# A planner that groups cache loads: later grouping, a constant for short transfers, and pairs for the free heads' values

## The chip, the core and the metric

The kernel runs on one core of one Trainium2 chip. The metric is device time in microseconds (us) of one execution. The core has TensorE (PE in the profile; its weight loads are listed apart as PEld), VectorE (DVE), ScalarE (ACT), GpSimd (POOL) and SyncE (SP). SP computes nothing here: it issues nearly all the transfers, one after the other, and waits before an issue until the place that the transfer will fill is free.

## What is computed

Four residual layers follow one another on eight sequences (batch rows) of one token each: attention over a cache, an MLP with a shift between the rows, and both again.

```python
x = A_x                                            # 8 rows of 448
x = x + A(layernorm(x), k_cache, v_cache, wq, wo)  # 16 query heads on 8 cached heads, 4096 keys, width 256
x = x + B(layernorm(x), w1, w2, w3, w4)            # MLP; also mixes neighbouring rows
x = x + A(layernorm(x), k_cache, v_cache, wq, wo)  # the same caches and weights
x = x + B(layernorm(x), w1, w2, w3, w4)
```

With one token in a row, the shift of B takes its values from outside the sequence, which are zeros; so every row goes through all four layers alone. A cached head of one row holds 4096 x 256 bf16 numbers, 2 MB for its keys and 2 MB for its values. All heads of all rows are 256 MB, and both attention layers need them.

## The kernel before, in words

**Tiles and places.** A head's keys or values lie in SBUF as four units ("quarters") of 512 KB, which are 4096 bytes in each of 128 partitions. `kv` has places for 30 quarters (`QUARTERS`), and everything streams through them. Heads 0 to 2 of a row are called free (`free_heads`): they are loaded afresh in each layer. Heads 3 to 7 are partly kept: of their keys 17 quarters, and of their values 7, stay in `kv` from the first attention layer to the second of the same row. 24 of 30 places are then taken, and six are left for the stream.

**Order of the work.** The row loop `for b in range(B)` interleaves the second layer of row b with the first layer of row b+1. For each row there is a stretch in which `mid` (the MLP of row b and the queries of its second layer) runs as a serial chain of small PE and DVE operations, while the values of the free heads of row b+1 pass through the six places. I call it the value stage. It comes seven times between rows, and the last rows end in a stretch of the same kind. After it the second layer's score operations (PE L1135) release kept keys, and more places come free.

**Operations of one quarter.** `front` transposes keys on PE (L1481, four at a time), copies them out of PSUM (DVE L1412 or ACT L1413) and scores them (L1135, or L1377 for whole rows of scores). `back` multiplies values with the softmax weights: eight matmuls of L1261 for a quarter, here called its PV. A quarter's last reader (the PV of a value quarter, the score of a key quarter) frees its place (`o.frees`).

**The planner.** `Plan.schedule` runs while the program is being built. It simulates all engines with costs in us and writes down one fixed instruction order for each. Nothing of it runs on the chip; on the chip each instruction waits on semaphores for those it depends on, and each engine takes its instructions in the written order. SP's order is fixed in advance (`prio`), but the planner decides how many neighbouring quarters of a head go in one transfer and which places they get. That is `next_kv`: `u.most` limits the group, it looks for a run of neighbouring free places of that length, and it accepts a later time for it up to

```python
late = max(free["sp"], dma_end - self.LEAD)
```

where `dma_end` is the planned end of all the transfers issued so far. When no such run comes in time, it takes the longest run that there is at that moment. A planned transfer starts at the earliest `ISSUE` = 4.0 us after its issue (`start = max(t + self.ISSUE, dma_end)`), and its duration is set in `issue_kv` (L644). The grouped transfer has one semaphore: the PV of its first quarter waits until the whole group has landed. A transfer for several places waits for the last of their former readers.

**Group limits.** In `back`, `most` is `MOST` for values of the free heads of rows 1 to 7 in the first layer, `MOST2` for one head of the second layer, and 4 otherwise. With `MOST = 1` the values of the free heads come as single quarters.

**Fillers.** Where the planned PE idles, the planner inserts matmuls without use (`warm`, L1686), if a count of recent columns is below a limit. There are 398 of them in the program.

Of the kernel before, what the change touches and what calls it, by code (L numbers as in the profile page):

```python
# [35 lines left out]
BOOST = None  # L36
HOTK = 7
L2 = (3, 4, 2, 1, 0)
MOST = 1
MOST2 = 4  # L40
BACKS = (0, 1, 3)
STAT_AT = 4
# [9 lines left out]
ST = 504  # L52
Q1 = 176
ROWS = True


class Op:
# [28 lines left out]
class Plan:  # L86
# [5 lines left out]
    HOT = 3500  # L92


    ISSUE, LEAD = 4.0, 5.0
    BLOCK, FETCH = 128, 6.0
    LAT = {"pe": 0.25, "dve": 0.06, "act": 0.06, "pool": 0.05, "sp": 0.4}

# [374 lines left out]
def bass_interleave_layers__gqa_block_cached__mixer_s_mlp__decode_kernel(  # L473
# [146 lines left out]
    FASTER = 1.05  # L620
# [15 lines left out]
    def issue_kv(o, n, q):  # L636

        (cache, b, h), u = o.unit.tile, o.unit.u
        src = cache[b, h].rearrange("(m s) d -> m (s d)", m=P)[:, u * 2048:(u + n) * 2048]
        dst = kv[:, q * 2048:(q + n) * 2048]  # L640
        slot_n[q] += 1
        o.emit = lambda eng: eng.dma_start(dst, src)
        o.dma = (slot_sem[q], 16 * slot_n[q])
        o.dur = ((n << 15) / 26.88e3 + 8 * 0.008) / FASTER  # L644

    plan.issue_kv = issue_kv

# [454 lines left out]
    def front(layer, b, h, prio=None):  # L1102
# [37 lines left out]
        def score_op(u, ss, where_of, keys):  # L1140
# [4 lines left out]
                           prio=prio and prio + len(plan.ops))  # L1145
        rows = ROWS and not last_head and not (layer and h == first2[b])
        by_rows[layer, b, h] = rows
# [87 lines left out]
    def back(layer, b, h):  # L1235
# [11 lines left out]
        fresh_v = [u for u in range(4) if u not in vs]  # L1247
        most = MOST if (layer == 0 and b and h in free_heads) else MOST2 if h == l2_heads[1] and layer else 4
        if (layer, b, h) == (1, B - 1, free_heads[-1]):
# [496 lines left out]
```

## Time and profile before

| | |
|---|---|
| three runs | 1083.20, 1088.74, 1092.21 us; median 1088.74 |
| profiled execution, its own time | 1083.66 us |
| its span, first to last instruction | 1081.5 us |
| mean granted TensorE clock | 0.923 |
| busy: PE, DVE, ACT, POOL | 944.7, 600.1, 338.3, 98.3 us |
| moved by DMA | 436.37 MB, mean 403 GB/s |
| transfers of `kv`: quarters, pairs, triples, fours | 219, 16, 15, 128 |

The last row adds up the key and value lines of the profile's list of DMA issues (512, 1024, 1536 and 2048 KB). A profile page cuts the span into 40 slices of 27 us and gives each the busy tenths of an engine, the granted clock and the moved GB/s. "To landing" is the time from the issue of a transfer by SP to the semaphore event that says that all of it has arrived; a transfer that stands behind others in the queue has a long one.

### The profile page before, as it was taken

How to read it: one execution, taken by the hardware profiler on the slowest of the kernel's cores; microseconds unless marked ns; L12 is line 12 of the kernel's file. 1: busy time of each engine (PE TensorE's matmuls, PEld its weight loads, DVE VectorE, ACT ScalarE, POOL GpSimd, SP SyncE). 2: the span in 40 equal slices, each digit the busy share in tenths (PEclk: the TensorE clock that was granted, in tenths of full speed). 3: DMA queues.
4: the chain of work that ended last, by engine and by line, in shares of the span. 5: the costliest groups of instructions: out<-in, count | busy, mean ns of one | idle time of the engine just before them, and what ended most of it. 6: DMA issues, size and time to landing. Idle time of an engine off the chain costs nothing.

```text
span 1081.5 us, 33945 instructions
## 1 busy us (share of the span) xinstructions
PE 944.7 (87%) x15116; PEld 650.5 (60%) x15116; DVE 600.1 (55%) x1896; ACT 338.3 (31%) x939; POOL 98.3 (9%) x278
## 2 busy tenths in 40 slices
PE   4988798998988988988999988889898898898795
PEld 3656556665656656666566665657565675566563
DVE  3345455554656556555565555565565665565564
ACT  1245023351223403353133421344122341243140
POOL 0000010000100101011010100000010000111010
PEclk9899989998999969999699998999899997999796
DMA  9999999999999999999999999999999999999994
GB/s 369 408 426 422 392 399 427 423 421 395 403 425 425 417 399 410 424 426 415 378 423 425 425 411 394 428 423 423 397 392 428 424 404 404 401 428 417 338 374 176
DMA packets 58973, 436.37 MB, mean 403 GB/s; under 512 B 6334, under 2 KB 9548, under 8 KB 38092
## 3 DMA queue, kind: packets, MB, share of 16 engines
q1 hardware_dynamic: 58740, 433.95, 98.0%
q8 instruction: 118, 1.93, 0.7%
q10 hardware_dynamic: 88, 0.26, 0.1%
q14 instruction: 27, 0.22, 0.1%
HBM read 434.18 MB, written 0.01 MB: 401 GB/s over the span
## 4 chain that ended last, share of the span: by engine, by line
DMA 52%; PE 37%; DVE 6%; issue 2%; ACT 1%; SPq 0%; POOL 0%; POOLq 0%; DVEq 0%
DMA kv<-in_A_k_cache_dram 32%; DMA kv<-in_A_v_cache_dram 19%; PE psT L1481 14%; PE psP L1261 7%; PE psT L1377 5%; PE psM L1135 3%; PE psR L1311 2%; PE psM L890 2%; DMA w3x_sb<-in_B_w_dram 1%; DVE oS L1277 1%; PE psP L1686 1%; DVE oS L1275 1%; DVE kv L1412 1%; PE psP L1285 1%; PE psM L1052 1%
## 5 line engine op out<-in xcount | busy, mean ns | idle before, releaser
L1481 PE MATMUL psT<-ident_f,kv 128*128 128x128 f32 x2752 | 381.6, 286 | 28.5 <-DMA kv<-in_A_k_cache_dram 26.5
L1481 PEld LDWEIGHTS psT<-ident_f,kv 128*128 128x128 f32 x2752 | 307.7, 145 | 109.6 <-issue 59.8
L1412 DVE COPY kv<-psT 128x512 f32<-128x512 f32 x377 | 258.4, 691 | 187.7 <-PE psT L1481 182.7
L1413 ACT COPY kv<-psT 128x512 f32<-128x512 f32 x343 | 199.9, 587 | 411.6 <-PE psT L1481 317.7
L1261 PE MATMUL psP<-kv,pT 128*2 128x256 bf16 x4096 | 181.2, 293 | 20.8 <-DMA kv<-in_A_v_cache_dram 18.4
L1377 PE MATMUL psT<-kv,qz 128*32 128x512 bf16 x1664 | 132.5, 394 | 4.3 <-ACT kv L1413 2.0
L1261 PEld LDWEIGHTS psP<-kv,pT 128*2 128x2 bf16 x4096 | 83.3, 83 | 66.2 <-DMA kv<-in_A_v_cache_dram 31.2
L1215 POOL PARTITION_ALL_REDUCE gm<-pm x128 | 45.5, 356 | 761.9 <-DVE pm L1213 748.0
L1225 ACT ACTIVATE pT<-sS,nb,fac 128x32 bf16<-128x32 bf16 x128 | 52.6, 417 | 96.8 <-DVE nb L1219 96.8
L1275 DVE CAST oS<-psP 128x256 bf16<-128x256 f32 x128 | 54.0, 422 | 49.9 <-PE psP L1261 48.6
L1311 PE MATMUL psR<-wo_sb,oT 128*1 128x448 bf16 x444 | 67.7, 389 | 4.3 <-DVE oT L1291 2.4
L1229 POOL PARTITION_ALL_REDUCE Db<-rs x128 | 51.2, 400 | 186.5 <-ACT pT L1225 186.5
L1285 PE MATMUL psP<-sel,oS 128*128 128x2 bf16 x512 | 32.1, 166 | 33.8 <-DVE oS L1277 32.1
L1285 PEld LDWEIGHTS psP<-sel,oS 128*128 128x128 bf16 x512 | 23.4, 99 | 63.4 <-DVE oS L1277 60.7
L1225 ACT ACTIVATE pT<-sS,nb 128x32 bf16<-128x32 bf16 x128 | 40.7, 325 | 58.9 <-DVE nb L1219 58.9
L1377 PEld LDWEIGHTS psT<-kv,qz 128*32 128x32 bf16 x1664 | 34.1, 95 | 39.2 <-issue 10.9
L1392 DVE CAST sr<-psT 128x512 bf16<-128x512 f32 x58 | 40.1, 691 | 29.4 <-PE psT L1377 29.1
L1277 DVE TENSOR_TENSOR oS<-psP,oS 128x256 bf16<-128x256 f32 x128 | 54.1, 423 | 3.2
L1686 PE MATMUL psP<-ident_f 128*128 128x256 bf16 x331 | 51.7, 283 | 0.0
L1135 PEld LDWEIGHTS psM<-qz,kv 128*128 128x128 bf16 x1344 | 41.9, 100 | 14.8 <-issue 5.4
L1135 PE MATMUL psM<-qz,kv 128*128 128x48 bf16 x1344 | 48.5, 188 | 1.4 <-DVE qz L1532 0.3
L1208 DVE CAST sS<-psM 128x64 bf16<-128x64 f32 x128 | 28.0, 219 | 33.4 <-PE psM L1135 25.7
(191 smaller groups left out, 777.2 us busy)
## 6 DMA issues: line engine op xcount, KB each, us to landing
kv<-in_A_k_cache_dram SPq DMA_DIRECT2D x68, 2048.0 KB, 23.0
kv<-in_A_v_cache_dram SPq DMA_DIRECT2D x60, 2048.0 KB, 17.2
kv<-in_A_v_cache_dram SPq DMA_DIRECT2D x182, 512.0 KB, 7.7
kv<-in_A_k_cache_dram SPq DMA_DIRECT2D x37, 512.0 KB, 7.8
kv<-in_A_k_cache_dram SPq DMA_DIRECT2D x11, 1536.0 KB, 17.8
kv<-in_A_v_cache_dram SPq DMA_DIRECT2D x11, 1024.0 KB, 8.7
kv<-in_A_v_cache_dram SPq DMA_DIRECT2D x4, 1536.0 KB, 9.9
kv<-in_A_k_cache_dram SPq DMA_DIRECT2D x5, 1024.0 KB, 9.6
```

What stands on the lines that cost most here:

```text
L1135: last = t.matmul(ps[:, SB + 2 * i:SB + 2 * i + 2 * REP], a()[:, c:256:2], bcast(rhs(c), REP, 1), start=(c == 0), stop=(c == 1))
L1225: return a.activation(pT[nr][:, :, :].rearrange("p i j -> p j i")[:, jj, :], sview[:, jj, :], ACT.Exp, bias=nb[nm][:, jj:jj + 1], scale=sc ...
L1261: last = t.matmul(ps[g4:g4 + 2, PV0:PV0 + DH], pT[nr][:, k, :], slot_ap(q, s * 256, 256), start=(i < 4), stop=(i >= 28), skip_group_check= ...
L1275: plan.op("dve", lambda v: v.tensor_copy(oS[:, 0, :], po), 0.36, "o", rd=[("pv", par, x) for x in range(4)], wr=["oS0"], banks=[bk], prio=hi)
L1277: plan.op("dve", lambda v: v.tensor_tensor(oS[:, 1, :], po, oS[:, 0, :], ALU.subtract), 0.36, "o", rd=["oS0"] + [("pv", par, x) for x in r ...
L1285: last = t.matmul(ps[:, PV1 + 2 * c:PV1 + 2 * c + 2], oS[:, w, c:DH:2], sel[:, :], start=(w == 0), stop=(w == 1))
L1311: last = t.matmul(psR[r:r + 1, 0:D], oT[no][:, i % 2, i // 2:i // 2 + 1], wo_sb[:, a:a + D], start=(k == 1 and i < 2), stop=(k == turn_at ...
L1377: last = t.matmul(psT[bank][32 * g:32 * g + 32, :], qz[:, a:a + 32], slot_ap(qs[g // 2], g % 2 * 1024, 1024)[:, c:1024:2], start=(half == ...
L1412: return e.tensor_copy(dst, psT[bank][:, :])
L1413: return e.copy(dst, psT[bank][:, :])
L1481: last = t.transpose(psT[bank][:, s * P:(s + 1) * P], src, ident_f[:, :])
L1686: return t.matmul(dst, ident_b, bcast(ident_b[:, 0:n // 4], 4, 1), start=True, stop=True)
```

## The change

Three numbers of the planner and the program are changed. `MOST` goes from 1 to 2, so that two quarters of a free head's values may go in one transfer. `LEAD` goes from 5.0 to 3.5, so that the planner waits for a longer run of free places until 3.5 us before the planned queue is empty. `SHORT`, a new constant of 0.1 us, is added to the planned duration of transfers of one or two quarters. No operation of the computation is added or taken away, and the bytes are the same; which quarters go together, the places, the order on all engines and the number of fillers follow from the planner.

```diff
-MOST = 1
+MOST = 2
 MOST2 = 4
...
 ROWS = True
+SHORT = 0.1
...
-    ISSUE, LEAD = 4.0, 5.0
+    ISSUE, LEAD = 4.0, 3.5
...
         o.emit = lambda eng: eng.dma_start(dst, src)
         o.dma = (slot_sem[q], 16 * slot_n[q])
-        o.dur = ((n << 15) / 26.88e3 + 8 * 0.008) / FASTER
+        o.dur = ((n << 15) / 26.88e3 + 8 * 0.008) / FASTER + SHORT * (n < 3)
```

## The prediction

> **What bounds the kernel now.** I read the page's slices and its DMA part first, then compared stretches, then looked at single waits.
>
> ```profile
> DMA  9999999999999999999999999999999999999994
> GB/s 369 408 426 422 392 399 427 423 421 395 403 425 425 417 399 410 424 426 415 378 423 425 425 411 394 428 423 423 397 392 428 424 404 404 401 428 417 338 374 176
> q1 hardware_dynamic: 58740, 433.95, 98.0%
> DMA 52%; PE 37%; DVE 6%; issue 2%; ACT 1%; SPq 0%; POOL 0%; POOLq 0%; DVEq 0%
> ```
>
> The DMA engines are busy from start to end, 98.0% of the span with SP's queue alone. PE's 37% of the chain that ended last is time in which a transfer was in flight too. So time is won or lost only where the stream slows: it moves 422 to 428 GB/s at best, and twice in about five slices it falls to some 395. The next view sets six value stages (262 to 916) beside four stretches of large transfers.
>
> ```profile
> 262.00:274.00 12.00, 11.48 (x236) 6.25 (x233) 7.36 (x41) 0.21 (x1) 0.00 (x0) 0.53 0.99 377
> 387.00:400.00 13.00, 12.12 (x260) 7.05 (x260) 7.01 (x41) 0.21 (x1) 0.00 (x0) 0.50 1.02 393
> 518.00:531.00 13.00, 12.26 (x258) 7.21 (x257) 7.42 (x42) 0.22 (x1) 0.00 (x0) 0.50 0.99 363
> 645.00:658.00 13.00, 11.24 (x266) 6.89 (x266) 7.17 (x42) 0.22 (x1) 0.00 (x0) 0.78 1.02 402
> 773.00:786.00 13.00, 11.70 (x262) 7.04 (x260) 6.81 (x40) 0.21 (x1) 0.00 (x0) 0.58 1.00 378
> 903.00:916.00 13.00, 12.29 (x273) 7.16 (x275) 6.92 (x41) 0.21 (x1) 0.00 (x0) 0.57 1.02 401
> ...
> 197.00:240.00 43.00, 40.22 (x438) 29.08 (x436) 24.67 (x59) 21.85 (x52) 4.13 (x11) 0.98 1.01 425
> 325.00:359.00 34.00, 30.60 (x346) 21.14 (x344) 22.09 (x53) 14.12 (x38) 3.38 (x9) 1.00 1.00 423
> 455.00:499.00 44.00, 40.09 (x447) 28.36 (x449) 24.99 (x60) 22.24 (x56) 4.36 (x12) 1.00 1.01 424
> 580.00:625.00 45.00, 42.08 (x468) 30.29 (x471) 25.81 (x64) 21.45 (x51) 4.06 (x11) 1.00 1.00 423
> ```
>
> The last three columns are granted clock, DMA share and GB/s. Weighted by length the value stages move 386 GB/s (363 to 402), the others 424. A quarter (0.524 MB) takes 1.36 us at the one rate and 1.24 at the other. The engines are not idle in the value stage (0.99 to 1.02); their packets are slower. PE has half its clock there in most windows.
>
> How full the queue is tells the time to landing: of the quarters issued in 387 to 400, then of all transfers of `kv`.
>
> ```profile
> DMA to landing us min/median/max: 6.5/6.7/7.2
> ...
> DMA to landing us min/median/max: 4.9/11.7/47.4
> ```
>
> The second line's 4.9 us is the shortest. Less a quarter's own 1.3 us (0.524 MB at 405 GB/s, below), some 3.6 us must lie queued ahead at its issue, or the stream has a hole. The stage has 6.7 - 1.3 = 5.4 us ahead: 1.8 us of cover. In the last stretch, 1003 to 1041, the cover fails:
>
> ```profile
> DMA  8979898999989999689999998312989999999999
> GB/s 280 289 285 293 293 276 250 410 375 401 388 293 341 306 289 302 267 358 392 392 431 423 440 384 345 121 56 60 224 233 332 388 336 388 418 401 427 423 423 474
> ```
>
> At 1027 to 1029 the engines fall to 1 to 3 tenths busy, while SP waits for a PV.
>
> **The change part by part.** The changed program's instruction order can be read without running it. It has 92 quarters, 57 pairs, 22 triples and 134 fours, 305 transfers for 378. So 127 quarter transfers go: 82 of these quarters come in pairs, 45 in triples and fours; the planner still finds no run of two places for many.
>
> *Size.* Between 124 and 134, where quarters stood deep in the queue (10.9 us to landing) at full clock, the stream made 405 GB/s: 1.295 us for a quarter, 0.056 over 1.239. I take that as the cost of being a quarter, the rest of 1.36 as that of a shallow queue. The pair's price is not seen apart; half-way, 0.028. Gain: 82 x 0.028 + 45 x 0.056 = **4.8 us**. The bounds: 0 if size costs nothing, and 127 x (1.358 - 1.239) = 15.1 us if all of the stage's slowness goes with size.
>
> The Trainium skill, DMA: Bandwidth & Descriptors, section Bandwidth, asks for transfers of at least 1 MiB for 75% of peak and gives 341 GB/s for one (measured with GpSimd issuing); an estimate from that page would price a quarter at over 1.54 us and raise the gain to some 38 us. The trace disagrees: queued quarters move 405.
>
> *Depth.* With six places, a quarter's issue waits for the PV of the quarter six before, so five quarters are ahead. In the old order 87 transfers wait with five ahead, three with four, one with three. In the new order 38 wait with five, 29 with four (18 of them pairs), three with three, one with two. One quarter less leaves 5.4 - 1.3 = 4.1 us ahead, 0.5 over the 3.6. A pair waits for two PVs, and at half clock 80 matmuls of L1261 took 6.3 us, 0.63 a quarter: 3.5 us ahead, no cover. The spread of the landing row is 0.7 us, so I price 0.2 us a pair and 0.05 a single: 18 x 0.2 + 11 x 0.05 = 4.1 us. Two pairs with three ahead lack a whole quarter: 2 x 1.3 = 2.6. Bounds: 0 (the 3.6 is an upper bound of what is needed) to the second rival's price.
>
> *The end.* At 386 GB/s the 12.55 MB of 1003 to 1041 would take 32.5 us instead of 38: 5.5 us lost to holes. The new order has its thinnest places there too (five ahead would be 6.5 us and are 5.4, so a release takes 1.1; two ahead are then 2.6 - 1.1 = 1.5 and lack 2.1 us, three ahead lack 0.8, and two waits behind transposes about 0.75 each): 4.4. Net -1.1, between -5.5 and +5.
>
> *Score waits.* At the end of each value stage the next quarters take places that scores (L1135) free. Before, each came when its own place was free; now a pair or triple waits for the last. SP's waits for L1135 are 73.1 us in 39 cases, 1.9 us each, under the queue. I price 0.5 us in each of seven stages, 3.5 in all, between 0 and two quarters' time, 2 x 1.3 x 7 = 18.2.
>
> *Fillers.* 488 instead of 398, 23 more in the value stages. The L1686 row has 283 ns or less for one. Outside the stages PE waits for DMA and they cost nothing; within, 23 x 0.283 = 6.5 us would be the price without cover. I take 1.
>
> *SP.* 73 issues less, about 0.33 us each, in the waiting time of an engine that computes nothing: 0. LEAD and SHORT run in no instruction; their effect is the order counted above. No other large part of the order changes: before, during and after, the fours of the key stretches have eight or more quarters ahead.
>
> Sum: -4.8 + 4.1 + 2.6 - 1.1 + 3.5 + 1 = **+5.3 us**. On the profiled execution's own 1083.66 (1081.5 of span) that is 1089.0. That execution lies at the low end of the three runs; on their median 1088.74 it is 1094.0. I forecast between: **1091 us**.
>
> **The rivals.**
> *Faster, the slowness goes with size.* Then 15.1 us return with no hole: 1068.6 by the execution, 1073.6 by the median; with half of it about 1079. For it: all slow slices are those with quarters. Against: quarters deep in the queue lost less than half of it, and the shallow stages have half the clock as well.
>
> *Slower, the queue runs dry.* Place: the pair's wait on two PVs in the value stage. It decides from the point where less than 3.6 us is queued ahead. If one PV more (0.63 us) is missing in each pair and half as much in each single: 18 x 0.63 + 11 x 0.3 = 14.6; with a whole quarter at each stage's score wait, 7 x 1.3 = 9.1, plus 2.6 and 1, less 4.8 and 1.1: +21.4, so 1105.1 by the execution and 1110 by the median. For it: the hole at 1027, and that PE is 86 to 96% busy in these stages at half clock. Against: the stage's landing times scatter by only 0.7 us. The Trainium skill (same page, Rules for kernel authors) says to issue a DMA early so that its fixed cost overlaps; pairs issue later, and by that rule this rival holds. The hole agrees with it.
>
> *The change hardly does what it says.* The order shows that it does in part; if pairs are as slow as quarters and the queue is still deep enough, it is the old time, within the forecast's class.
>
> **How the numbers follow.** A measurement of this kernel can tell about 1% (10.9 us) from no change. Forecast and the unchanged case, 1078 to 1099.6: 0.53. Queue dry, above: 0.32. Size, below: 0.15. The range takes most of both: 1077 to 1108.
>
> **What would show it.** Right: the list of issues with 92 quarters; value stages near 386 GB/s still; shortest landing of pairs near 3.6 + 2.5 us with small holes in the slices; the key stretches at 424. Size right: 405 or more in the value stages. Dry: DMA digits below 9 in each stage and long waits of SP for L1261 and L1135. Wrong altogether: a key stretch below 420, or a chain that ends on PE while the DMA idles.

## The result, and the profile after

The changed kernel takes 1095.36 us (median of 20 runs, 1089.34 to 1099.50), the kernel before beside it 1086.53 us (20 runs). The ratio is 1.0079, with a 95% interval of 1.0063 to 1.0094: some 8.6 us slower, within the 1% that the prediction called "same". The profiled execution has a span of 1094.1 us against 1081.5, which is 12.6 us; 4 us of that difference belong to these two executions and not to the kernels, so the accounting below, which is made on the two traces, explains more than the medians ask for.

First the slices, the queue and the chain of the changed kernel's page.

```profile
DMA  9999999999999999999999999999999999999894
GB/s 367 409 425 422 390 378 425 425 417 378 405 427 425 419 359 412 427 424 417 371 426 424 423 401 377 428 424 416 384 409 425 425 407 346 422 424 409 303 380 180
q1 hardware_dynamic: 48228, 433.95, 97.1%
DMA 53%; PE 34%; DVE 6%; SPq 4%; issue 1%; ACT 1%; POOL 0%; DVEq 0%
```

The best slices move 422 to 428 GB/s, as they did. The slow slices have become slower: 359, 371 and 346 stand where 399, 378 and 404 stood. A new entry in the chain is SP's queue with 4% (0 before); it is no measure of the loss, for `SHORT` alone (below) has 5% there without one, and experiment 5, which lost more, has 0%. The windows show where the time went. Six value stages stand first, four key stretches after them; the last three columns are again the granted clock, the DMA share and GB/s.

```profile
262.00:276.00 14.00, 13.49 (x296) 8.87 (x293) 7.03 (x42) 0.21 (x1) 0.00 (x0) 0.56 0.96 338
390.00:404.00 14.00, 13.30 (x281) 8.51 (x280) 7.19 (x43) 0.21 (x1) 0.00 (x0) 0.51 0.95 333
521.00:535.00 14.00, 13.49 (x293) 8.77 (x290) 7.13 (x42) 0.21 (x1) 0.00 (x0) 0.55 0.98 349
650.00:664.00 14.00, 13.82 (x295) 9.02 (x288) 7.24 (x42) 0.21 (x1) 0.00 (x0) 0.64 0.96 355
780.00:794.00 14.00, 13.09 (x301) 8.73 (x293) 7.36 (x43) 0.21 (x1) 0.00 (x0) 0.65 0.97 348
910.00:924.00 14.00, 12.94 (x322) 9.16 (x323) 7.32 (x42) 0.21 (x1) 0.00 (x0) 0.88 0.89 323
199.00:242.00 43.00, 40.03 (x440) 28.87 (x438) 24.31 (x60) 22.61 (x56) 4.24 (x12) 1.00 1.00 423
328.00:361.00 33.00, 30.23 (x345) 21.09 (x344) 22.10 (x53) 13.69 (x35) 3.36 (x9) 1.00 1.01 425
459.00:502.00 43.00, 38.69 (x426) 27.20 (x425) 23.61 (x58) 21.52 (x52) 4.12 (x11) 1.00 1.00 423
585.00:630.00 45.00, 40.56 (x445) 29.74 (x443) 23.88 (x58) 20.71 (x50) 3.76 (x10) 0.96 1.00 423
```

The key stretches are what they were (423 to 425). The value stages fell from a mean of 386 GB/s to 341, and their DMA share from 0.99 to 1.02 down to 0.89 to 0.98: before, the packets were slow but the engines never idle; now the engines idle as well. One stage seen closely, 388 to 417, in 40 slices of 0.7 us:

```profile
DMA  9999879899979989699999898999999999999998
GB/s 384 446 373 412 333 271 277 362 395 463 305 226 373 373 339 339 249 328 350 316 345 260 294 384 271 356 418 390 379 429 345 379 458 362 345 401 424 367 441 356
```

There is no single hole, but nine small ones: 6 to 8 tenths busy again and again. The same view of the kernel before (385 to 412) shows 9 in all slices but one. The times to landing, of the transfers issued in 390 to 404 and then of all of `kv`, say the same:

```profile
DMA to landing us min/median/max: 5.4/6.4/7.4
...
DMA to landing us min/median/max: 4.0/13.3/47.6
```

The shortest landing fell from 4.9 to 4.0 us. In 390 to 404 three pairs (median 6.9 us) and four quarters (6.0) are listed. Less the pair's own 2.5 us, a pair has 4.4 us ahead of it; the stage before had 5.4. The list of issues has 92 quarters (72 of values, 20 of keys), as the order said.

**An account of the stream.** A transfer's landing less the landing of the one before it is its spacing. Where more than 6 us are queued ahead, the median spacing is 1.273 us for a quarter, 2.49 for a pair, 3.72 for a triple and 4.909 for a four, which is 1.227 for each of its quarters. What a transfer lands later than that I call its hole. It is "thin" where less than 5.2 us were queued ahead at its issue, and belongs to a PV or a score by the operation that the written order makes it wait for. Loads of weights that land between two transfers of `kv` are no hole. In us, from issue and landing times of the two traces (number of transfers in brackets):

| | before | after | difference |
|---|---|---|---|
| size: median spacings over 1.227 a quarter | 11.3 | 7.2 | -4.1 |
| thin, PV, value stages to 1003 us | 0.8 (8) | 18.6 (41) | +17.8 |
| thin, score, up to 1003 us | 2.0 (11) | 1.9 (6) | -0.1 |
| thin, from 1003 us to the end | 5.5 (4) | 10.1 (6) | +4.6 |
| all others | 25.4 | 19.2 | -6.2 |
| sum | 45.1 | 57.1 | +12.0 |

The sum is 12.0 of the 12.6 us of span. The last row is mostly number as well: a transfer with more than 6 us queued ahead lands some 0.06 us later on average than at the median, in both kernels (17.5 us in 273 transfers, 12.1 in 224), and there are fewer of them. With mean spacings in place of medians (1.321, 2.509, 3.766, 4.989) the size row is -8.6, and the last row is smaller in the same measure.

### The profile page after: what moved, and what is told of

The parts are those of the page before. It is cut to its first block, busy times and chain, and to the rows that moved or that the text cites. A ratio compares the mean times of both kernels' runs of the same rounds, so it can differ in the third digit from the quotient of the medians.

```text
span 1094.1 us, 34048 instructions
## 1 busy us (share of the span) xinstructions
PE 946.7 (87%) x15206; PEld 654.1 (60%) x15206; DVE 596.8 (55%) x1891; ACT 342.3 (31%) x944; POOL 97.9 (9%) x278
## 3 DMA queue, kind: packets, MB, share of 16 engines
q8 instruction: 119, 1.95, 0.7%
## 4 chain that ended last, share of the span: by engine, by line
DMA 53%; PE 34%; DVE 6%; SPq 4%; issue 1%; ACT 1%; POOL 0%; DVEq 0%
DMA kv<-in_A_k_cache_dram 31%; DMA kv<-in_A_v_cache_dram 22%; PE psT L1482 10%; PE psP L1262 7%; PE psT L1378 4%; SPq L643 4%; PE psM L1136 3%; PE psR L1312 2%; PE psM L891 2%; PE psP L1687 1%; DVE oS L1276 1%; DVE oS L1278 1%; PE psM L1053 1%; SPq L626 1%; PE psP L1286 1%
## 5 line engine op out<-in xcount | busy, mean ns | idle before, releaser
L1482 PE MATMUL psT<-ident_f,kv 128*128 128x128 f32 x2752 | 371.3, 282 | 27.6 <-DMA kv<-in_A_k_cache_dram 25.4
L1482 PEld LDWEIGHTS psT<-ident_f,kv 128*128 128x128 f32 x2752 | 301.3, 143 | 107.0 <-issue 53.4
L1413 DVE COPY kv<-psT 128x512 f32<-128x512 f32 x371 | 254.9, 690 | 191.5 <-PE psT L1482 184.0
L1414 ACT COPY kv<-psT 128x512 f32<-128x512 f32 x349 | 203.8, 586 | 383.8 <-PE psT L1482 298.6
L1262 PE MATMUL psP<-kv,pT 128*2 128x256 bf16 x4096 | 176.1, 290 | 22.3 <-DMA kv<-in_A_v_cache_dram 19.1
L1378 PE MATMUL psT<-kv,qz 128*32 128x512 bf16 x1664 | 133.4, 392 | 5.5 <-ACT kv L1414 2.2
L1262 PEld LDWEIGHTS psP<-kv,pT 128*2 128x2 bf16 x4096 | 88.5, 85 | 67.1 <-DMA kv<-in_A_v_cache_dram 27.3
L1687 PE MATMUL psP<-ident_f 128*128 128x256 bf16 x414 | 70.4, 291 | 2.4 <-DVE oT L1292 1.3
L1312 PE MATMUL psR<-wo_sb,oT 128*1 128x448 bf16 x444 | 63.8, 371 | 8.8 <-DVE oT L1292 3.9
L1286 PEld LDWEIGHTS psP<-sel,oS 128*128 128x128 bf16 x512 | 23.2, 98 | 65.6 <-DVE oS L1278 62.0
L1286 PE MATMUL psP<-sel,oS 128*128 128x2 bf16 x512 | 32.2, 167 | 34.2 <-DVE oS L1278 32.2
L1378 PEld LDWEIGHTS psT<-kv,qz 128*32 128x32 bf16 x1664 | 34.6, 95 | 38.5 <-issue 10.9
L1136 PE MATMUL psM<-qz,kv 128*128 128x48 bf16 x1344 | 47.6, 187 | 3.4 <-DVE kv L1413 2.8
L1136 PEld LDWEIGHTS psM<-qz,kv 128*128 128x128 bf16 x1344 | 41.2, 99 | 14.8 <-DVE kv L1413 4.5
L1687 PEld LDWEIGHTS psP<-ident_f 128*128 128x128 bf16 x414 | 34.5, 100 | 20.7 <-issue 14.3
## 6 DMA issues: line engine op xcount, KB each, us to landing
kv<-in_A_k_cache_dram SPq DMA_DIRECT2D x10, 1536.0 KB, 17.8
```

Source lines behind the costliest of these rows:

```text
L1136: last = t.matmul(ps[:, SB + 2 * i:SB + 2 * i + 2 * REP], a()[:, c:256:2], bcast(rhs(c), REP, 1), start=(c == 0), stop=(c == 1))
L1262: last = t.matmul(ps[g4:g4 + 2, PV0:PV0 + DH], pT[nr][:, k, :], slot_ap(q, s * 256, 256), start=(i < 4), stop=(i >= 28), skip_group_check= ...
L1286: last = t.matmul(ps[:, PV1 + 2 * c:PV1 + 2 * c + 2], oS[:, w, c:DH:2], sel[:, :], start=(w == 0), stop=(w == 1))
L1312: last = t.matmul(psR[r:r + 1, 0:D], oT[no][:, i % 2, i // 2:i // 2 + 1], wo_sb[:, a:a + D], start=(k == 1 and i < 2), stop=(k == turn_at ...
L1378: last = t.matmul(psT[bank][32 * g:32 * g + 32, :], qz[:, a:a + 32], slot_ap(qs[g // 2], g % 2 * 1024, 1024)[:, c:1024:2], start=(half == ...
L1413: return e.tensor_copy(dst, psT[bank][:, :])
```

## The experiments

All ratios are to the kernel before, run beside it on the same chip, with a 95% interval. `plan.schedule()` has written all orders when the edits of the first, second, third, fifth and ninth experiment run; they change the written order and not the planner.

**1. The kernel before, each quarter one PV later.** Where a quarter's issue waits for a PV with five quarters ahead, it also waits for the next PV.

```diff
     plan.schedule()
+    turns = [o for o in plan.order["pe"] if o.name == "pv"]
...
+        if mine and nxt and at[o][1] - mine[0][2] == 5 and nxt[0][0] < at[o][0]:
+            o.deps[turns[i + 1]] = False
     plan.synchronise()
```

> The kernel before, with its order, places and sizes kept; only 89 transfers that had five quarters queued ahead wait for one more PV, so that 85 quarters have four ahead. Theory depth (a transfer with four quarters or fewer ahead leaves holes in the stream): the changed kernel lost about 12.6 us of span plus the 4.8 us that size should have given on some 33 such transfers, 0.5 us each; here 85 of them, though neighbours share a hole: +12 to +35 us, ratio 1.011 to 1.032, holes in every value stage. Theory order (the new instruction order on PE costs the time, the queue's depth does not): within 2 us of before, ratio 0.998 to 1.002.

Measured: 1.0338 (1.0310 to 1.0367), span 1118.8 us; thin holes (under 5 us ahead, the first transfer of all counted in) 48.6 us where before has 9.5. The dose was impure: for eight of the 89 transfers the next PV stands behind a block of scores on PE, and the landings fall back 4 to 8 us at once near the end of a stage. The run shows that depth can cost much more than forecast, not what one quarter of depth costs. Experiment 9 repeats it without these eight.

**2. After, its pairs and triples taken apart.** Places and PE's order are those of after; each pair and triple is issued as single quarters, each with its own wait and its own semaphore (272 quarters, 134 fours).

```diff
     plan.schedule()
+    for o in plan.order["sp"]:
+        split.append(o)
+        parts = o.parts
+        if 1 < len(parts) < 4:
...
+    plan.order["sp"] = split
     plan.synchronise()
```

> The changed kernel with its PE order and places kept; every pair and triple is taken apart into quarters again, each waiting for its own place alone: 272 quarters and 134 fours, six quarters with four ahead, 71 with five. Theory depth: the holes go (about -12 us against the changed kernel) and 101 more transfers cost some 4 us: ratio to before 0.998 to 1.004. Theory order: the loss stays, and the size gain goes too: 1.008 to 1.013.

Measured: 1.0128 (1.0102 to 1.0154), span 1101.4 us: slower than after, not faster. The pair's wait for two PVs is therefore not what lost most of the time. Two value stages of this run:

```profile
523.00:537.00 14.00, 12.86 (x275) 8.41 (x273) 7.22 (x41) 0.21 (x1) 0.00 (x0) 0.50 0.94 326
653.00:667.00 14.00, 13.38 (x274) 8.72 (x267) 6.05 (x34) 0.21 (x1) 0.00 (x0) 0.50 0.97 338
```

They are as thin as after's. Of 62 quarters that wait with five ahead, the median issue comes about 2.3 us after the landing of the data that the awaited PV reads, against 0.85 us before. So the lateness sits in the written order of PE, which this run shares with after. The thin holes at PVs are 14.1 us up to 1003 us (after 18.6), and from there to the end 5.5 (after 10.1): a part went with the pairs. And 101 transfers more cost 1.0128 - 1.0079 = 0.0049, which is 5.3 us or 0.053 us each (some 0.02 to 0.085 by the two intervals). This is a net figure: the same step took 11 us of thin holes away, so a transfer by itself costs more.

**3. After, without the fillers of the value stages** (93 matmuls of L1687 dropped).

```diff
+        if o.name == "warm" and stage:
+            DROPPED.append(o)
+            continue
```

> The changed kernel without the 93 filler matmuls that stand in its value stages; all else is the same. Theory depth: the same as the changed kernel within 2 us, ratio 1.006 to 1.010. Theory fillers (they delay the PVs of the value stage at half clock): up to 6.5 us less and more if they sit before PVs: 1.000 to 1.003.

Measured: 1.0086 (1.0056 to 1.0117). The fillers cost nothing that is measured.

**4, 6, 7 and 10. One part alone, and LEAD undone.**

```diff
-MOST = 1
+MOST = 2
```

> The kernel before with MOST = 2 alone (LEAD 5.0, no constant): 189 quarters, 34 pairs, 17 triples, 125 fours; 13 quarters with four ahead, two with three, one each with two and one. Theory depth: 17 thin transfers against four in before, 13 x 0.5 us, less 13 x 0.05 for fewer transfers: about +6 us, ratio 1.003 to 1.008. If pairs as such paid (size), 0.995 to 0.999.

```diff
-    ISSUE, LEAD = 4.0, 5.0
+    ISSUE, LEAD = 4.0, 3.5
```

> The kernel before with LEAD = 3.5 alone: 168 quarters, 23 pairs, 18 triples, 135 fours; 14 transfers with four ahead, one each with three and two. Theory thin queue (0.45 us for each such transfer, as the one-later-PV kernel showed: 36 us for 85; size pays 0.05 us for each transfer saved): 12 more thin ones, +5.4, 34 fewer transfers, -1.7: +4 us, 1.003. Rival planned pace (LEAD below ISSUE makes the planner believe in holes, and PE's order follows it; this is the part that costs): 1.006 to 1.010, as the whole change.

```diff
+SHORT = 0.1
...
-        o.dur = ((n << 15) / 26.88e3 + 8 * 0.008) / FASTER
+        o.dur = ((n << 15) / 26.88e3 + 8 * 0.008) / FASTER + SHORT * (n < 3)
```

> The kernel before with the constant SHORT = 0.1 alone: 200 quarters, 24 pairs, 20 triples, 125 fours; thin transfers 5 against 4 in before, one of them with only one quarter ahead. Theory thin queue: +1 to +3 us for the two thinnest, -0.5 for size: 1.000 to 1.003. Rival planned pace (a planned stage that is longer than the real one by 0.1 us per transfer costs as a later order on PE): 1.003 to 1.006.

Pairs and the constant, with `LEAD` at 5.0:

> The changed kernel with LEAD back at 5.0: 154 quarters, 44 pairs, 10 triples, 134 fours; 19 transfers with four or fewer ahead. If the three parts add up (pairs alone 1.0030, LEAD alone 1.0063, the constant alone 0.9988, together 1.0081 against 1.0079 measured): 1.001 to 1.003. If pairs and LEAD need each other to cost: 0.997 to 1.000. If pairs and the constant make it: 1.005 or more.

| | ratio | thin holes (under 5.2 us ahead), us: PV, score |
|---|---|---|
| pairs alone | 1.0030 (1.0010 to 1.0049) | 6.1, 9.1 |
| `LEAD` alone | 1.0063 (1.0037 to 1.0089) | 14.2, 9.4 |
| `SHORT` alone | 0.9988 (0.9967 to 1.0008) | 7.9, 1.7 |
| pairs and `SHORT` | 1.0017 (0.9997 to 1.0036) | 14.9, 2.0 |
| all (after) | 1.0079 (1.0063 to 1.0094) | 26.4, 4.3 |
| none (before) | 1 | 6.3, 2.1 |

`LEAD` carries most of the loss. Its 1.0063 lies where the expectation's rival, the planned pace, had put it, above the 1.003 of the thin queue counted by quarters; experiment 8 tests that rival. The parts add up to 0.30 + 0.63 - 0.12 = 0.81%, against 0.79% measured: within these intervals (0.2 to 0.3 each) the effects on the time add. The holes don't: `LEAD` alone adds 7.9 us at PVs and 7.3 at scores, added to pairs and `SHORT` it adds 11.5 and 2.3. Each version is another order, with its own thin places. Pairs alone lose much in one spot near the end, as 40 slices of 1010 to 1048 us show:

```profile
DMA  9999899999999999999951000076858989999999
GB/s 328 427 267 220 341 410 401 414 418 418 418 379 410 405 423 410 448 397 401 401 224 69 26 9 0 17 168 254 259 172 190 285 280 392 401 444 379 431 448 431
```

The hole lies at 1029 to 1035 us: the landings are 2.5 us behind those of before ahead of it and 7.0 us behind after it.

**5. After, PVs earlier on PE.** The 93 fillers are dropped, and each PV of a value stage moves ahead of up to two operations of the MLP chain or of the output sums (82 of the chain, 35 others).

```diff
+        i, left = kept.index(o), 2
+        while left and kept[i - 1].name in ("chain", "wor", "osum"):
...
+            kept[i - 1], kept[i] = o, p
```

> The changed kernel, sizes, places and waits kept, without the 93 value-stage fillers; on PE each value-stage PV is moved ahead of up to two neighbouring operations of the MLP chain or the output projection (82 chain blocks, 18 and 17 others). Theory late release (the written order puts PVs of pairs behind blocks of the chain, so places come free 1.8 to 2.4 us after landing instead of 1.1): most of the 0.8% returns: ratio 0.999 to 1.004. Rival ahead (a pair has four quarters ahead whatever PE does): 1.006 to 1.009. If moving makes the chain itself late, the loss turns up at the score waits instead: 1.008 to 1.015.

Measured: 1.0158 (1.0134 to 1.0183), span 1101.5 us, just above the third branch. The releases did come earlier (about 1.1 us after the data's landing with four ahead, 1.8 in after; 1.4 against 2.1 with five), and yet the time grew. What SP waits for, first in after and then here (total us, times, longest; L1378 and L1136 are the scores, L1286 an operation of the output sums):

```profile
SPq L643 <- PE psP L1262: 538.9, 116, 25.4
SPq L643 <- PE psT L1378: 224.0, 46, 19.6
SPq L643 <- PE psM L1136: 62.9, 22, 7.4
SPq L643 <- PE psP L1286: 36.1, 25, 9.0
```

```profile
SPq L645 <- PE psP L1264: 509.3, 114, 25.7
SPq L645 <- PE psT L1380: 223.1, 46, 19.3
SPq L645 <- PE psM L1138: 70.1, 23, 8.1
SPq L645 <- PE psP L1288: 69.8, 24, 9.9
```

The view names the operation that ended last, and here that misleads: in the written order no transfer waits for an output sum, so the waits at L1286 and L1288 belong to PVs and scores. Added up from the trace by what the written order makes SP wait for, the waits for PVs are 551.1 us in after and 550.8 here, those for the scores of L1136 and L1138 75.0 and 83.3. The thin holes of score waits up to 1003 us rose from 1.9 to 13.2 us, those of PVs hardly fell (18.6 to 17.5). The first score of the next layer, which frees kept places, comes 16.7 us after the last kept value has landed (median of seven stages), in after 15.7; but in before it is 16.8, so this delay by itself does not make the loss. Nor is PE full here: without the fillers it is 71 to 86% busy in 14 us of six value stages, where in after it is 92 to 99% busy, at a granted clock of 0.51 to 0.88. That the chain loses what the PVs gain, because both take turns on one engine, fits the score waits but is argued, not shown.

**8. After, planned with a shorter issue.** A planned transfer starts at the earliest 2.5 us after its issue, not 4.0.

```diff
-    ISSUE, LEAD = 4.0, 3.5
+    ISSUE, LEAD = 2.5, 3.5
```

> The changed kernel with ISSUE = 2.5 in the planner instead of 4.0, so that a wait up to LEAD = 3.5 leaves no planned hole: 112 quarters, 51 pairs, 22 triples, 132 fours; 30 transfers with four or fewer ahead against 33. Theory thin queue counted by quarters ahead: about the changed kernel, 1.005 to 1.010. Rival planned pace: PE's order fits the real stream better, and half or more of the loss returns: 0.999 to 1.004.

Measured: 1.0084 (1.0058 to 1.0110); thin holes 18.3 us at PVs and 10.9 at scores. That the holes were planned, by a pace that the planner thinks free, is not borne out; the run can't exclude it, since the whole order differs.

**9. Before, each quarter one PV later, without the eight of experiment 1 that stood behind scores.**

```diff
+        between = [p.name for p in plan.order["pe"][turns[i].pos:turns[i + 1].pos]]
...
+                not {"sc", "scr"} & set(between):
+            o.deps[turns[i + 1]] = False
```

> The kernel with one later PV again, but without the eight waits whose next PV stands behind a block of score operations on PE; 81 transfers wait for a PV that follows soon after, so that 79 have four quarters ahead where they had five, with PE's order, places and sizes of the kernel before. Theory ahead (four instead of five is what costs, 0.43 us each): +30 us or more, 1.028 to 1.034. Theory late release (one quarter less costs little as long as the PV comes 0.85 us after landing; the eight waits behind scores made the 3.4%): +3 to +10 us, 1.003 to 1.009.

Measured: 1.0078 (1.0056 to 1.0099), 8.5 us for 79 quarters that now have four ahead: 0.11 us each (0.08 to 0.14 by the interval). Their release is as prompt as before (0.72 us after the landing), and 4.63 us are queued ahead of them, 1 us over the 3.6 that the prediction took as needed. One stage, 385 to 412 us, in 40 slices:

```profile
DMA  9999999998898889989999999999999989998999
GB/s 455 382 395 401 425 401 419 413 413 358 261 388 316 310 334 388 310 297 255 309 382 431 394 401 407 419 388 407 401 413 394 310 328 370 425 346 273 285 346 388
```

This is a milder form of the look of after's stages, with the old order on PE, all quarters single and only the depth less. A quarter of depth by itself makes small holes: that is shown.

**11. Before, seven places.** `KEEP_V = 6` keeps one quarter less of the values, so the stream has a place more and 8 more quarters to load (9.8 us at 1.227).

```diff
-KEEP_V = 7
+KEEP_V = 6
```

> The kernel before with KEEP_V = 6: one value quarter less is kept for each row and is loaded again, eight more quarters (816), 9.8 us more of stream at 428 GB/s; in return the value stages have seven places instead of six, and only four transfers wait with five or fewer ahead behind a PV in a value stage, against 91. Theory thin queue: the 13 us of holes that before has at less than 5.2 us queued ahead mostly go, so -3 to +4 us, 0.997 to 1.004. If before's holes have another cause: +9.8 us, 1.008 to 1.011.

Measured: 1.0036 (1.0014 to 1.0057), 3.9 us for 9.8 us of transfers; about 6 us came back (4 to 8 by the interval; in the profiled execution, with 1088.2 us of span, 3). The stage's time to landing is 8.8 us. The 13 us of the expectation counted as a hole 3.9 us in which MLP weights landed between two quarters; without them the thin holes are 8.4 us before and 6.0 here, and those up to 1003 us, at PVs and scores, go from 2.9 to nothing. Depth helps from the other side too, and does not pay for its bytes.

**12. Before, `LEAD` further the other way.**

```diff
-    ISSUE, LEAD = 4.0, 5.0
+    ISSUE, LEAD = 4.0, 7.0
```

> The kernel before with LEAD = 7.0 for 5.0 and nothing else. Its written order has 395 transfers of keys and values for 378, and 90 waits with at most five quarters ahead for 91 (LEAD 3.5: 344 transfers, 88 waits, 14 of them with four for 3). Theory that the depth and lateness of the waits carry the loss of LEAD 3.5: the thin waits are as many as before, 17 more transfers cost 17 x 0.053 = 0.9 us; ratio to before 0.998 to 1.004, holes of transfers with under 5 us ahead within 4 us of the 9.5 of before. Rival, that the loss goes with LEAD itself, so that a planner that groups earlier goes on gaining: 1.5 us of LEAD lost 6.8 us, so 2 us the other way give some 9 back; ratio 0.990 to 0.995. Third: two thinnest places (one and two quarters ahead, where before has none) open holes of up to 2 x 3 us; ratio 1.004 to 1.007, and the loss is seen at those two places.

Measured: 1.0044 (1.0026 to 1.0062), the third branch. The span is 1091.2 us, 9.7 over that of before. Up to 1016 us the landings are 5 us behind, and the other half is lost at one of the two thinnest places. Forty slices of 1000 to 1040 us:

```profile
DMA  9999999998985978799999899999999720000009
GB/s 385 426 393 418 410 406 422 389 324 336 410 336 209 283 262 266 225 352 373 381 365 315 287 410 397 418 422 414 430 389 397 287 98 29 20 0 0 0 0 160
```

For 7 us, from 1032 on, nearly nothing moves: SP has waited 13.4 us for one PV, and the quarter issued at 1038.24 finds the queue empty since 2.9 us. A longer wait for runs lost time and so did a shorter one; the number of `LEAD` is not a direction to go in.

## Why the prediction was right, and where its steps were not

**The class and the sign.** 1091 us were forecast, 1077 to 1108 as the range; 1095.36 was measured. Worked from the terms, +5.3 us stood against some +8.6. The sign, the place (the value stages) and the quiet key stretches came as the working had them, but two of its terms were far off and partly cancelled others.

**Size: right in kind, from a mixed stretch.** -4.8 us forecast; -4.1 by median spacings, -8.6 by mean ones, and 0.053 us net for each transfer less by experiment 2. The half-way price of a pair (0.028 saved a quarter) was near by the medians, (2 x 1.273 - 2.491) / 2 = 0.028, and low by the means, 0.067. The stretch from 124 to 134 us, read as quarters alone, holds four loads of MLP weights that land between 129.0 and 132.9 us; the quarters around them land 1.27 to 1.30 us apart, so a quarter costs 0.046 us over a four's share by the medians, not 0.056. With the size term the rival "the slowness goes with size" (1073.6, or 1079) fell. The Trainium skill, DMA: Bandwidth & Descriptors, section Bandwidth, would have a gain of some 38 us, the prediction's estimate from its figure for transfers of 1 MiB; the traces disagree, and the measured 4 to 9 us decide for a queue that holds other transfers ahead.

**Depth: the term that failed, 6.7 us for 17.8.** The step put 0.2 us on a pair and 0.05 on a single with four ahead and 2.6 us on two pairs with three. Two things in it were wrong.

The first is the price of a quarter of depth. "One quarter less leaves 4.1 us ahead, 0.5 over the 3.6" makes a single nearly free; experiment 9 measured 0.11 us at 4.63 us ahead. The 3.6 was an upper bound of what a transfer needs, read as if the stream were whole above it. There is no such point in the traces (last section).

The second is lateness. The working took a release of 1.1 us after the landing from the stage before, and added one PV (0.63 us) for a pair. In after the release takes about 1.8 us (28 transfers with four ahead, 3.9 us queued) and 2.1 us (28 with five, not the 38 that the working counted, 5.3 us queued), and experiment 2 shows the lateness with no pair in it. It comes from the order on PE. Here are six entries of PE's order in a stage before, then five of after (start, duration, line, count; L1261 and L1262 are PVs, L1052 and L1053 the second part of the MLP):

```profile
392.82 0.60 PE L1261 MATMUL psP<-kv,pT 128*2 128x256 bf16 x8 [0.29 <-DMA kv<-in_A_v_cache_dram]
393.35 0.92 PE L1052 MATMUL psM<-hT,w_sb 128*128 128x12 bf16 x28
394.19 0.60 PE L1261 MATMUL psP<-kv,pT 128*2 128x256 bf16 x8
394.72 0.89 PE L1052 MATMUL psM<-hT,w_sb 128*128 128x12 bf16 x27
395.54 0.22 PE L1076 MATMUL psM<-hT,w_sb 128*64 128x12 bf16 x1
395.69 0.60 PE L1261 MATMUL psP<-kv,pT 128*2 128x256 bf16 x8
```

```profile
397.65 0.60 PE L1262 MATMUL psP<-kv,pT 128*2 128x256 bf16 x8
398.18 1.26 PE L1053 MATMUL psM<-hT,w_sb 128*128 128x12 bf16 x41
399.37 0.22 PE L1077 MATMUL psM<-hT,w_sb 128*64 128x12 bf16 x1
399.53 0.54 PE L1053 MATMUL psM<-hT,w_sb 128*128 128x12 bf16 x14
400.00 1.02 PE L1262 MATMUL psP<-kv,pT 128*2 128x256 bf16 x16
```

Before, a PV comes every 0.9 to 1.5 us with at most one block of the chain between. After, the pair that landed at 398.32 waits 1.7 us behind 2 us of the chain, and then both its PVs run in one piece; the places come free in bursts. The planner has grouped the quarters and, with them, the work on PE. Experiment 5 shows that this is no slip to be mended by moving the PVs forward: then the holes come at the scores. What is shown is that depth alone makes holes (9), that the lateness is there without pairs (2), and that pushing it out costs more (5). Of after's 18.6 us, 12.5 are holes of transfers with four quarters ahead and 3.8 of those with five. How the 17.8 us divide between lateness and the quarter less is not measured. By experiment 9's price the 28 transfers with four ahead would make 3.1 us, an estimate from that run alone, so lateness would have the larger share.

**Score waits: 3.5 us forecast, -0.1 measured up to 1003 us.** In after the holes lie at PVs. But `LEAD` alone, which groups transfers in the same way, has 9.4 us there up to 1003 (before 2.0): the mechanism exists, in another of the orders.

**The end: -1.1 us forecast.** The step's 5.5 us lost before and its 4.4 after turned out as 5.5 and 10.1 in holes; by the landings, which also carry the gain of size, after is 10.4 us behind at 1003 and 12.6 at the last transfer, +2.2. The thin places named were the right ones; three ahead lacked more than 0.8 us.

**Fillers: 1 us forecast, 0 measured (3).** PE is 92 to 99% busy in the stages and 83 to 94% without the fillers; most of them seem to stand where it waits anyway.

**The rivals.** "The queue runs dry" had the right place and mechanism, thin queues in each value stage, with 1105 to 1110 us a larger price; its condition, less than 3.6 us ahead, is met by 9 of after's 28 transfers with four ahead. By the rule of the Trainium skill (DMA: Bandwidth & Descriptors, section Rules for kernel authors) to issue a DMA early it was to hold; experiments 9 and 11 agree in sign, from both sides. "The change hardly does what it says" fell with `LEAD` alone at 1.0063.

**What is open.** Why holes appear with 3 to 5 us still queued ahead; why the loss of `LEAD` lies half at scores without pairs and mostly at PVs with them; whether the planned pace has a part in it.

## What to carry to other kernels

Where a stream is fed through few places, the cost of a transfer is less its size (0.053 us net for each here) than how much is still queued when it is issued, and that is set by the engine that frees the places: compare the time from landing to the next issue, and the us queued ahead, ahead of counting transfers. A planner's constant that regroups transfers rewrites the order of every engine; test it on both sides, as here 3.5 and 7.0 both lost to 5.0, and look for the one or two thin places of each order, since a single wait can be worth half of the difference. Of several constants changed together, try each alone: the constant for short transfers alone came out at 0.9988 (0.9967 to 1.0008), not to be told from no change, while the whole lost 0.8%.

## What the runs showed of the hardware that was not expected

A stream that has work queued still slows, gradually. The mean hole of a transfer in after, by what was queued ahead at its issue:

| us queued ahead | under 3 | 3 to 4 | 4 to 5 | 5 to 6 | over 6 |
|---|---|---|---|---|---|
| mean hole, us | 1.2 | 0.68 | 0.34 | 0.19 | 0.05 |
| transfers | 8 | 19 | 22 | 26 | 224 |

The first 10 us of the execution are left out. I had expected a sharp point near 3.6 us. The shortest landing, 4.0 us for a transfer that takes 1.3 in the stream, says that about 2.7 us can be enough, and yet the loss is there at 5. Whether single DMA engines run empty earlier than others, for example those that carry the instruction packets of the page's part on queues (119 of them, 1.95 MB), was not tried.
